# Attention times a gated dense block on one Trainium2 core: products with values in three blocks a pair of heads instead of four

## The chip, the cores and the metric

The kernel runs on one core of a Trainium2 chip. A core has a matrix engine (TensorE, PE in the profile, with PEld for its weight loads), a vector engine (VectorE, DVE), an engine for activations (ScalarE, ACT), a general one (GpSimd, POOL) and SyncE (SP), from whose queue all transfers of this kernel are issued. Each engine works through its own instructions in order. The metric is the device time of one execution in microseconds (us); lower is better.

## The reference

The input x has 2048 rows of 640 numbers. It is normalized row by row, and the result goes into two branches whose outputs are multiplied:

```python
xn = _layernorm(x, axis=-1)
s = _A_ref(xn, A_wqkv, A_wo)                               # attention
g = _silu(_B_ref(xn, B_w1, B_b1, B_w2, B_b2))              # dense block
return x + s * g
...
# attention: H = 32 heads of Dh = 20, window W = 256
mask = (idx[:, None] - idx[None, :] >= 0) & (idx[:, None] - idx[None, :] < W)
p = _softmax(jnp.where(mask, q @ k.T * Dh ** -0.5, -1e9))
return (p @ v).reshape(B, S, D) @ wo
# dense block: 640 -> 1536 -> 640
r = max(xn @ w1 + b1, 0)
return (r * r) @ w2 + b2
```

All data are 32-bit floats. With a window of 256, a tile of 128 queries meets three tiles of 128 keys: its own and the two before it.

## The kernel before

**Precision by parts.** Matrix products run in a reduced 32-bit form, so most operands are split into a high and a low part and three products are added (high x high, high x low, low x high).

**Three stages.** The first normalizes and transposes x, computes the values v for all heads and the first 128 columns of q and k, and stores them in device memory. The second is a loop of *steps* (line 1186), which does attention and, between its products, nearly everything else. The third multiplies the attention result with `wo`, gates it and writes the output (`out_filler`, line 1114).

**Steps.** Heads go in 16 pairs, each pair through 16 tiles of 128 rows. Step `s` computes the scores of one tile of queries (`scores`, line 470) and their row maxima on VectorE (`maxima`, line 482). Every fourth step the maxima of four tiles are turned on TensorE, negated and stored into two extra rows of q (`max_rows`, line 488). `LAG` = 9 steps later the same scores are computed transposed, keys by queries, with the maxima subtracted by those rows (`scores_t`, line 510); ScalarE takes the exponential and GpSimd sets the part outside the window to zero with one or two masks (`exps`, line 522, instructions on lines 524, 525 and 527). This leaves one probability tile for each block of keys `kb`, kept in `pts` in a ring of 8 buffers (tag `p32`).

**Products with values.** `PLAG` steps after the exponentials of the fourth, eighth, twelfth and sixteenth tile of a pair, `values(p, g)` (line 532) multiplies the last four probability tiles with v. The results of 8 tiles of queries lie in one accumulator `ot` of four column groups; two tiles share a column group, and a block of keys adds to up to three tiles. A 21st column of ones beside v's 20 columns gives the sums of the softmax. `evac` then copies two column groups to SBUF (line 551) and posts one store into `o_d[g]` (line 552); posted stores are issued by `post_all` (line 564) from SyncE's queue, which waits there for the copy.

**Two streams and the filler.** Score products and nearly all others in the loop use only 64 of the 128 rows of TensorE, so two of them run side by side: the code keeps two streams with a model clock each (`clock[0]`, `clock[1]`), puts the first half of a product into one and its second half into the other. The value products use all 128 rows, so `values` brings both clocks together and adds `PV`, the time the code books for a block. Between the products of attention, a generator `filler` (line 827) emits the rest: q and k for the other heads, then the first layer (`hps`) and the second layer (`yps`) of the dense block. `fill(upto)` (line 1166) takes work from it until the model clock has come to a given point. `pace` (line 1164) is all booked work divided by the number of steps, and each step fills up to `(s + 1) * pace`, or to `(s + 1) * pace - PV` where a block of values follows (line 1226).

**The order at the end.** The last block of the second layer consists of 8 half-products: four tiles of rows, each in two halves of 320 columns, one bank of three for each. VectorE empties a bank (`ysb`, line 960). Ahead of each half-product the filler calls `late()` (line 878), which, counted by `j`, loads the first attention results back (`load`, line 1062: transfers `ob` and `sums`), and turns them into operands (`turn_out`, line 1077: VectorE and ScalarE). The inverse of the softmax sums comes from `invert` (line 1019), called in every step: from `stored(g) + 3` on it loads the sums of column group `g`, from `stored(g) + 5` on VectorE takes the reciprocal, and a transfer stores it. `tick` (line 718) releases the splitting of weights (ScalarE line 765 or 773, VectorE line 768 or 774) by step and by how loaded the step is taken to be.

Of the kernel before, what the change touches and what calls it, by code (L numbers as in the profile page):

```python
# [9 lines left out]
F32 = mybir.dt.float32  # L10
# [5 lines left out]
P = 128  # L16
# [8 lines left out]
NB = 4  # L25
# [14 lines left out]
WARM2 = 10  # L40
COST = {P: 0.067, 2 * P: 0.12, HALF: 0.147, 3 * P: 0.172, BT: 0.23}
SCALE = DH ** -0.5
PV = 1.57
PLAG = 2
NEG = -1.0e30
EPS = 1e-5
SETTLE = 0.45
# [10 lines left out]
def attn_mlp_kernel(ctx: ExitStack, tc, x, wqkv, wo, w1, b1, w2, b2, out):  # L58
# [470 lines left out]

    ot = po_.tile([P, 4, P], F32, tag="o", name="ops")  # L530

    def values(p, g):
        for kb in range(4 * g, 4 * g + 4):
            pt = pts.pop((p, kb))
            ts = range(kb, min(kb + 3, NT))
            same, other = [t for t in ts if t % 2 == kb % 2], [t for t in ts if t % 2 != kb % 2]
            parts = [same] if kb % 8 < 6 else [[t] for t in same]
            for part in parts + [other]:
                for hh in range(2):
                    if not part:  # L540
                        continue
                    t = part[0]
                    r0 = 32 * (2 * hh + t % 2)
                    c0 = t // 2 % 4
                    first = t % 8 < 2 and kb == max(0, t - 2) or kb == 0
                    nc.tensor.matmul(ot[r0:r0 + VW, c0:c0 + len(part), :], vps[p][:, kb // 4, kb % 4, hh, :], pt[:, hh, :].rearrange("p (t n) -> p t n", n=P)[:, t - kb:part[-1] - kb + 1:2, :], start=first, stop=part[0] == kb, skip_group_check=True)  # L546
        clock[:2] = [max(clock[:2]) + PV] * 2

        def evac():
            osb = at2.tile([P, 2, P], F32, tag="osb", name="osb")  # L550
            nc.scalar.activation(osb, ot[:, 2 * g % 4:2 * g % 4 + 2, :], AF.Copy)
            post(o_d[g][p], osb.rearrange("p e n -> p (e n)"))
        later(SOON, evac)


# [271 lines left out]
    def filler():  # L827
# [50 lines left out]
        def late():  # L878
            j = lates[0]
            lates[0] += 1  # L880
            if j >= 3:
                load(0)
            if j >= 4:
                load(1)
            if j >= 5:
                turn_out(0, 0)
            if j >= 6:
                turn_out(0, 1)
                load(2)

# [118 lines left out]
        return 4 * (u // 2) + u % 2 + 2 * t2  # L1009

    def stored(g):
        return NP * NT - NT + 4 * g + 3 + LAG + PLAG

    rec_d = [dram.tile([2, H, MT], F32, name=f"rec_{g}") for g in range(NB)]
    recs = {}
# [3 lines left out]
    def invert():  # L1019
        for g in range(NB):  # L1020
            over = state[2] >= 10 ** 6
            if not over and state[2] < stored(g) + 3:
                return
            if g not in recs:
                rows = o_d[g].rearrange("p (h r) n -> (p h) r n", h=2)
                recs[g] = at2.tile([P, P], F32, tag="rec", name="rec")
                for par in range(2):
                    nc.sync.dma_start(recs[g][64 * par:64 * (par + 1)], rows[:, 32 * par + DH].rearrange("h (j n) -> h j n", n=P))
            elif recs[g] is not None and (state[2] >= stored(g) + 5 if not over else True):
                nc.vector.reciprocal(recs[g], recs[g])  # L1030
                nc.sync.dma_start(rec_d[g].rearrange("a h (j n) -> (a h j) n", n=P), recs[g])
                recs[g] = None
# [128 lines left out]
    whole = [False]  # L1161
    fl = filler()
    steps = NP * NT + LAG + PLAG
    pace = (8 * (KC - 1) * 15 * COST[BT] + 4 * NB * (3 * 30 * COST[MT] + 4 * 18 * COST[HALF]) + NP * (2 * NT * COST[3 * P] + NB * PV)) / (steps - 1)

    def fill(upto):
        soon()
# [10 lines left out]
    with tc.manual_schedule(engines={E_.PE, E_.Activation, E_.DVE, E_.Pool, E_.SP}):  # L1178
# [7 lines left out]
        for s in range(steps):  # L1186
# [35 lines left out]
            issue(RATE)  # L1222
            flush()
            tick()
            if e and e[1] % 4 == 3:
                fill((s + 1) * pace - PV)
                values(e[0], e[1] // 4)
            else:
                fill((s + 1) * pace)
        finish()  # L1230
# [30 lines left out]
```

## Time and profile before

| What | Value |
|---|---|
| Median of 3 runs | 863.55 us (861.12 to 864.31) |
| Profiled execution | 860.56 us, of which 858.8 us are the span from first to last instruction |
| TensorE busy | 845.2 us, 98% of the span |
| VectorE, ScalarE, GpSimd busy | 455.7, 423.2, 323.0 us |
| Clock granted to TensorE | full over the whole span |
| Value products | 2112, in 64 blocks |
| Stretches of the span | first stage to about 150 us; steps with q and k to 268 us; steps with the dense block to 784 us; output products from 784 us |

How to read it: a "busy" engine has an instruction running; products are pipelined on TensorE, so their records overlap and a busy TensorE can still be fed more or less densely. In the order of time, each row gives start, length, engine, line, operation, what is written and read, and the count of instructions merged into the row. What stands in brackets is the idle time before it and what ended it. Names are those of the program: `ops` is the accumulator of the value products, `p` a probability tile, `sps` and `stps` the two forms of scores, `hps` and `yps` the two layers of the dense block, `wops` the output products, `osb` the copy of the attention result.

### The profile page before, as it was taken

What the parts mean: (1) busy time and instruction counts of PE and PEld (TensorE: products, weight loads), DVE (VectorE), ACT (ScalarE), POOL (GpSimd) and SP (SyncE); (2) the same over time, 40 slices, a digit from 0 to 9 for tenths busy, and PEclk for the clock granted to TensorE, in tenths of its full rate; (3) what the DMA queues carried; (4) which work ended last, traced back from release to release, by engine and by line L of the source; (5) the groups of instructions that cost most, each with busy time, mean ns of one, the idle gap of its engine ahead of it and who ended that gap; (6) DMA issues with size and microseconds to landing.
All of it is one profiled execution on the core that took longest, in us unless ns stands there. A gap on an engine that the chain in (4) does not pass through costs nothing. (4 is left out here: it accounts for less than half of the span.)

```text
span 858.8 us, 26512 instructions
## 1 busy us (share of the span) xinstructions
PE 845.2 (98%) x10640; PEld 790.8 (92%) x10640; DVE 455.7 (53%) x1348; ACT 423.2 (49%) x808; POOL 323.0 (38%) x652
## 2 busy tenths in 40 slices
PE   9999999999999999999999999999999999979998
PEld 8999999888888999999999989999999999979997
DVE  7652136655567545454455456655445455345764
ACT  5222114545556753753754654854744744752321
POOL 6010002333333543543543543643543543621443
PEclk9999999999999999999999999999999999999999
DMA  7998587877879563264265336485276284367992
GB/s 264 297 405 292 169 210 259 272 246 251 267 252 300 145 209 125 77 193 129 80 201 179 89 101 180 128 261 173 71 209 180 66 256 143 95 141 205 281 269 85
DMA packets 94371, 166.50 MB, mean 194 GB/s; under 512 B 10920, under 2 KB 43816, under 8 KB 93224
## 3 DMA queue, kind: packets, MB, share of 16 engines
q1 hardware_dynamic: 94248, 164.80, 62.7%
q8 instruction: 84, 1.38, 0.7%
q14 instruction: 39, 0.32, 0.1%
HBM read 93.66 MB, written 70.52 MB: 191 GB/s over the span
## 5 line engine op out<-in xcount | busy, mean ns | idle before, releaser
L486 DVE CUSTOM_DVE_ANT_0 junk<-sps,mask 128x384 bf16<-128x384 f32 (+2 forms) x512 | 272.5, 532 | 249.0 <-PE hps L468 71.9
L524 ACT ACTIVATE p<-stps 128x768 f32<-128x768 f32 (+2 forms) x256 | 197.3, 771 | 261.9 <-PE stps L518 211.8
L468 PE MATMUL yps<-w,hh 64*128 64x320 f32 x1536 | 230.1, 309 | 6.6 <-DVE ysb L960 6.2
L525 POOL TENSOR_SCALAR_AFFINE_SELECT p<-p 128x256 f32<-128x256 f32 x256 | 104.3, 407 | 333.7 <-ACT p L524 319.2
L468 PE MATMUL hps<-xb,w 64*128 64x256 f32 x2520 | 220.7, 283 | 0.0
L468 PEld LDWEIGHTS hps<-xb,w 64*128 64x128 f32 x2520 | 208.8, 187 | 5.5 <-issue 5.4
L468 PEld LDWEIGHTS yps<-w,hh 64*128 64x128 f32 x1536 | 186.0, 185 | 11.6 <-DVE ysb L960 8.0
L468 PE MATMUL yps<-w,hl 64*128 64x320 f32 x768 | 178.5, 310 | 0.0
L478 PE MATMUL sps<-ks,qs 60*128 60x384 f32 (+2 forms) x512 | 142.6, 341 | 0.2
L518 PE MATMUL stps<-qs,ks 62*128 62x384 f32 (+2 forms) x512 | 135.6, 331 | 0.0
L468 PEld LDWEIGHTS yps<-w,hl 64*128 64x128 f32 x768 | 117.7, 185 | 2.3 <-issue 2.3
L468 PE MATMUL qkps<-xT,wgkh 64*128 64x512 f32 x320 | 100.5, 395 | 0.0
L468 PE MATMUL qkps<-xT,wgqh 64*128 64x512 f32 x320 | 98.9, 393 | 0.0
L546 PE MATMUL ops<-p,vp 128*21 128x128 f32 (+1 forms) x2112 | 92.8, 313 | 0.0
L527 POOL TENSOR_SCALAR_AFFINE_SELECT p<-p 128x256 f32<-128x256 f32 x224 | 91.5, 409 | 0.0
L478 PEld LDWEIGHTS sps<-ks,qs 60*128 60x128 f32 x512 | 87.7, 185 | 2.6 <-DVE mt L486 1.3
L518 PEld LDWEIGHTS stps<-qs,ks 62*128 62x128 f32 x512 | 88.5, 187 | 0.4
L546 PEld LDWEIGHTS ops<-p,vp 128*21 128x21 f32 x2112 | 65.2, 100 | 22.0 <-issue 8.8
L228 PE MATMUL vps<-wv,xT 128*128 128x320 f32 x480 | 71.5, 308 | 0.0
L228 PEld LDWEIGHTS vps<-wv,xT 128*128 128x128 f32 x480 | 70.5, 188 | 0.1
L930 POOL TENSOR_TENSOR hl<-sq,hh 128x512 fp32r<-128x512 f32 x48 | 62.3, 1298 | 21.2 <-ACT sq L929 21.2
L599 PE MATMUL wops<-wo,oT 128*128 128x320 f32 x384 | 61.6, 309 | 0.7 <-DVE ysb L960 0.7
(104 smaller groups left out, 1167.5 us busy)
## 6 DMA issues: line engine op xcount, KB each, us to landing
ks<-k_d SPq DMA_DIRECT2D x64, 240.0 KB
qs<-q_d SPq DMA_DIRECT2D x64, 240.0 KB
xb<-xs SPq DMA_DIRECT2D x60, 256.0 KB
xs<-xT SPq DMA_DIRECT2D x8, 1280.0 KB
k_d<-shm SPq DMA_DIRECT2D x19, 512.0 KB
q_d<-shm SPq DMA_DIRECT2D x19, 512.0 KB
y<-ysb SPq DMA_DIRECT2D x28, 320.0 KB
o<-osb SPq DMA_DIRECT2D x64, 128.0 KB
```

Source lines behind the costliest of these rows:

```text
L228: nc.tensor.matmul(ps, xT[xp][b][:, c * BT + t * P: c * BT + (t + 1) * P], wv[wp][:, c, nh * HALF:(nh + 1) * HALF], start=first and m == 0 ...
L468: return nc.tensor.matmul(out, a[r], b_[r], skip_group_check=True, **kw)
L478: nc.tensor.matmul(ss[hh][:, :nk], qs[i][o, q * P:(q + 1) * P], ks[i][o, k0 * P:k0 * P + nk], start=True, stop=True)
L486: nc.vector.tensor_tensor_reduce(out=junk[:, :nk], in0=ss[hh][:, :nk], in1=mask[:, 3 * P - nk:], scale=1.0, scalar=-3.0e38, op0=ALU.add, o ...
L518: nc.tensor.matmul(tps[:, hh, :n], ks[i][o, kb * P:(kb + 1) * P], qs[i][o, kb * P:kb * P + n], start=True, stop=True)
L524: nc.scalar.activation(p32[:, :, :n], tps[:, :, :n], AF.Exp, scale=SCALE)
L525: nc.gpsimd.affine_select(p32[:, :, 0:P], p32[:, :, 0:P], pattern=[[0, 2], [1, P]], compare_op=ALU.is_ge, fill=0.0, base=0, channel_multip ...
L527: nc.gpsimd.affine_select(p32[:, :, 2 * P:], p32[:, :, 2 * P:], pattern=[[0, 2], [-1, P]], compare_op=ALU.is_gt, fill=0.0, base=0, channel ...
L546: nc.tensor.matmul(ot[r0:r0 + VW, c0:c0 + len(part), :], vps[p][:, kb // 4, kb % 4, hh, :], pt[:, hh, :].rearrange("p (t n) -> p t n", n=P ...
L599: nc.tensor.matmul(ps, a, b_, start=j == 0, stop=j == n - 1)
L930: nc.gpsimd.tensor_sub(hh[1][:, :BT], sq, f32(hh[0]))
```

## The change

The 16 probability tiles of a pair are multiplied with v in three blocks, of six, six and four, instead of four blocks of four, and a block runs one step behind the exponentials of its last tile instead of two. With it go:

- the copy out takes three, three and two column groups; the second of these wraps around the end of the accumulator and becomes two copies; stores are cut where the column groups belong to different `o_d[g]`, so a pair has five stores instead of four;
- the time booked for a block is 2.25, 2.25 and 1.42 us instead of 1.57;
- `stored(g)` and the steps from which `invert` acts are set anew, the buffer of the inverted sums becomes single, and a new inversion starts only when none is open;
- `late()` acts at other counts of half-products.

```diff
-PV = 1.57
-PLAG = 2
+CUTS = (0, 6, 12, NT)
+PVS = (2.25, 2.25, 1.42)
+PLAG = 1
...
-    def values(p, g):
-        for kb in range(4 * g, 4 * g + 4):
+    def values(p, i):
+        lo, hi = CUTS[i], CUTS[i + 1]
+        for kb in range(lo, hi):
...
-        clock[:2] = [max(clock[:2]) + PV] * 2
+        clock[:2] = [max(clock[:2]) + PVS[i]] * 2
 
         def evac():
-            osb = at2.tile([P, 2, P], F32, tag="osb", name="osb")
-            nc.scalar.activation(osb, ot[:, 2 * g % 4:2 * g % 4 + 2, :], AF.Copy)
-            post(o_d[g][p], osb.rearrange("p e n -> p (e n)"))
+            c0, c1 = lo // 2, hi // 2
+            osb = at2.tile([P, 3, P], F32, tag="osb", name="osb")
+            c = c0
+            while c < c1:
+                n = min(4 - c % 4, c1 - c)
+                nc.scalar.activation(osb[:, c - c0:c - c0 + n], ot[:, c % 4:c % 4 + n, :], AF.Copy)
+                c += n
+            for g in range(c0 // 2, (c1 + 1) // 2):
+                d0, d1 = max(c0, 2 * g), min(c1, 2 * g + 2)
+                post(o_d[g][p, :, (d0 - 2 * g) * P:(d1 - 2 * g) * P], osb[:, d0 - c0:d1 - c0].rearrange("p e n -> p (e n)"))
...
-            if j >= 3:
+            if j >= 4:
                 load(0)
-            if j >= 4:
                 load(1)
-            if j >= 5:
+            if j >= 6:
                 turn_out(0, 0)
-            if j >= 6:
+            if j >= 7:
                 turn_out(0, 1)
                 load(2)
...
-        return NP * NT - NT + 4 * g + 3 + LAG + PLAG
+        return NP * NT - NT + min(c for c in CUTS if c >= 4 * (g + 1)) - 1 + LAG + PLAG
...
-            if not over and state[2] < stored(g) + 3:
+            if not over and state[2] < stored(g) + 2:
                 return
             if g not in recs:
+                if any(r is not None for r in recs.values()):
+                    return
                 rows = o_d[g].rearrange("p (h r) n -> (p h) r n", h=2)
-                recs[g] = at2.tile([P, P], F32, tag="rec", name="rec")
+                recs[g] = at2.tile([P, P], F32, tag="rec", bufs=1, name="rec")
...
-            elif recs[g] is not None and (state[2] >= stored(g) + 5 if not over else True):
+            elif recs[g] is not None and (state[2] >= stored(g) + 4 if not over else True):
...
-            if e and e[1] % 4 == 3:
-                fill((s + 1) * pace - PV)
-                values(e[0], e[1] // 4)
+            if e and e[1] + 1 in CUTS:
+                i = CUTS.index(e[1] + 1) - 1
+                fill((s + 1) * pace - PVS[i])
+                values(e[0], i)
```

More of the change, by code (lines that the diff above doesn't have):

```diff
@@ L1163, in attn_mlp_kernel @@
     steps = NP * NT + LAG + PLAG
-    pace = (8 * (KC - 1) * 15 * COST[BT] + 4 * NB * (3 * 30 * COST[MT] + 4 * 18 * COST[HALF]) + NP * (2 * NT * COST[3 * P] + NB * PV)) / (steps - 1)
+    pace = (8 * (KC - 1) * 15 * COST[BT] + 4 * NB * (3 * 30 * COST[MT] + 4 * 18 * COST[HALF]) + NP * (2 * NT * COST[3 * P] + sum(PVS))) / (steps - 1)
     def fill(upto):
```

## The prediction

> **What bounds the kernel now.** I read the page first (shares, clock, chain, costliest groups), then the busy time by stretch, then TensorE's instructions in order of time around blocks of value products, then the waits near the end.
>
> ```profile
> span 858.8 us, 26512 instructions
> PE 845.2 (98%) x10640; PEld 790.8 (92%) x10640; DVE 455.7 (53%) x1348; ACT 423.2 (49%) x808; POOL 323.0 (38%) x652
> PEclk9999999999999999999999999999999999999999
> PE 9%; DVE 0%; issue 0%
> PE wops L599 8%; PE yps L468 1%; PE ops L546 0%; DVE res L1151 0%; DVE ysb L960 0%; DVE res L1153 0%
> L546 PE MATMUL ops<-p,vp 128*21 128x128 f32 (+1 forms) x2112 | 92.8, 313 | 0.0
> ```
> ```profile
> 268.00:735.00 467.00, 465.14 (x7188) 437.49 (x7186) 245.69 (x841) 270.86 (x528) 212.49 (x447) 1.00 0.52 154
> 735.00:784.00 49.00, 43.38 (x621) 40.16 (x618) 18.02 (x36) 26.16 (x47) 16.38 (x31) 1.00 0.59 154
> 784.00:858.80 74.80, 70.56 (x480) 70.30 (x480) 46.57 (x64) 19.12 (x28) 31.26 (x30) 1.00 0.74 208
> ```
>
> TensorE (PE) is busy 98% of the span at full clock, and in the long middle, 268 to 735 us, for 465.14 of 467.00 us (first column the length, second PE, then weight loads, VectorE, ScalarE, GpSimd). No engine beside it is over 53%. So time is gained here only by making TensorE's stream shorter, and lost only by making TensorE wait. "Busy" hides one thing that the change is about: how densely products follow each other. For that I go to the order of time, one step without values and one with a block:
>
> ```profile
> 736.69 0.34 PE L478 MATMUL sps<-ks,qs 60*128 60x384 f32 x1
> ...
> 737.16 2.15 PE L468 MATMUL hps<-xb,w 64*128 64x256 f32 x32
> 739.08 0.34 PE L478 MATMUL sps<-ks,qs 60*128 60x384 f32 x1
> ...
> 739.26 0.34 PE L518 MATMUL stps<-qs,ks 62*128 62x384 f32 x1
> ...
> 739.55 0.71 PE L468 MATMUL hps<-xb,w 64*128 64x256 f32 x8
> 740.19 1.50 PE L546 MATMUL ops<-p,vp 128*21 128x256 f32 x32
> 741.62 0.38 PE L468 MATMUL hps<-xb,w 64*128 64x256 f32 x1
> 741.63 0.44 PE L478 MATMUL sps<-ks,qs 60*128 60x384 f32 x1
> 741.84 0.28 PE L468 MATMUL hps<-xb,w 64*128 64x256 f32 x1
> 741.91 0.34 PE L518 MATMUL stps<-qs,ks 62*128 62x384 f32 x1
> 741.96 0.34 PE L478 MATMUL sps<-ks,qs 60*128 60x384 f32 x1
> 742.09 0.28 PE L468 MATMUL hps<-xb,w 64*128 64x256 f32 x1
> 742.14 0.34 PE L518 MATMUL stps<-qs,ks 62*128 62x384 f32 x1
> 742.21 1.94 PE L468 MATMUL hps<-xb,w 64*128 64x256 f32 x28
> ```
>
> Columns: start, length, engine, line, operation, count. Ordinary products use 64 of the 128 rows each, two streams side by side; the value products (L546) use all 128 rows and 21 columns. In a plain run 32 products of 256 columns start within 2.15 - 0.28 = 1.87 us, 0.060 us apart. From 736.69 to 737.16 lie four score products and two of these: (0.47 - 0.12) / 4 = 0.088 us a score product.
>
> **The price of a block's edges.** From 739.55 to 742.21, 2.66 us, TensorE does 8 + 3 products of 256 columns (11 x 0.060 = 0.66), four score products (0.35) and one block: the block takes 2.66 - 1.01 = 1.65 us. Its 32 products start within 1.50 - 0.27 = 1.23 us, 0.040 apart, so 32 cost 1.27. The rest, 0.38 us, is paid for going into the full-row form and back: 0.21 us from the start of the last ordinary product (739.55 + 0.71 - 0.28 = 739.98) to 740.19, 0.20 us from the last value product's start (741.42) to 741.62, and 741.62 to 742.21, 0.59 us for work that goes in 0.53 elsewhere. A lower bound takes only the two gaps, less what an ordinary and a value product would need (0.41 - 0.10 = 0.31), less 0.06 because both streams restart together: 0.25 us. I take 0.35, near the upper row, since that one counts everything from the last undisturbed product to the next, and keep 0.25 to 0.38.
>
> [...]
>
> **The change part by part.**
> Blocks: 48 instead of 64 over 16 pairs; the 2112 value products, their weights and shapes stay. 16 x 0.35 = 5.6 us less on the engine that is the bound (4.0 to 6.1).
>
> One step behind instead of two: a block's last probabilities must be ready one step sooner. What that needs, once as usual and once the worst of the last steps of a block to be (6th, 12th, 16th of a pair):
>
> ```profile
> 346.57 0.34 PE L518 MATMUL stps<-qs,ks 62*128 62x384 f32 x1
> 348.40 0.41 POOL L527 TENSOR_SCALAR_AFFINE_SELECT p<-p 128x256 f32<-128x256 f32 x1
> 349.24 0.34 PE L518 MATMUL stps<-qs,ks 62*128 62x384 f32 x1
> ...
> 544.20 0.48 PE L518 MATMUL stps<-qs,ks 62*128 62x384 f32 x2
> 546.85 0.98 POOL L527 TENSOR_SCALAR_AFFINE_SELECT p<-p 128x256 f32<-128x256 f32 x1
> 546.93 0.34 PE L518 MATMUL stps<-qs,ks 62*128 62x384 f32 x1
> ```
>
> Usually GpSimd's second mask ends at 348.81, 2.24 us after the scores began at 346.57. A block starts 740.19 - 739.26 = 0.93 us behind its step's scores; one step later that is 349.24 + 0.93 = 350.17, so 1.36 us to spare. The worst is ready at 547.83, wanted at 547.86. And a block goes through its steps in order: of 48 products the last step's come after 40, another 40 x 0.04 = 1.6 us. Waiting of TensorE: 0; if that cover went, every late microsecond would cost one per block, 48 times. A block now holds seven probability tiles at its start (six of its own, one newer) where six were held, of eight buffers, so the exponentials wait for none.
>
> ScalarE, SyncE, planner:
>
> ```profile
> L551 ACT ACTIVATE osb<-ops 128x256 f32<-128x256 f32 x64 | 24.3, 379 | 5.6 <-PE ops L546 5.6
> L524 ACT ACTIVATE p<-stps 128x512 f32<-128x512 f32 x16 | 9.6, 599 | 28.1 <-PE stps L518 28.1
> L564 SPq DMA_DIRECT2D o<-osb x64: 319/343/666, 154.9 to 777.8; - x64
> SPq L564 <- ACT osb L551: 189.9, 54, 7.0
> ```
>
> Copies out stay 64: one of three column groups, one of one, two of two a pair. By 0.38 us for 256 columns and 0.60 for 512, 384 columns are about 0.49 and 128 about 0.27 (estimates), together 1.52 a pair against 4 x 0.38 = 1.52: 0. Stores rise from 64 to 80, 16 x 0.34 = 5.5 us on SyncE, which in that queue waits 189.9 us for these copies anyway: 0. Queued behind a block's second store is at times the pair of row stores for the maxima; their readers come three steps (over 7 us) later, so 0.34 us more is covered. The planner books 2.25 us for six steps; such a step then lasts some 0.96 + 2.25 = 3.2 us instead of 2.4 and the next carries less filler. The work is the same, and the rows show no wait that depends on even steps: 0. One step fewer in all, and a filler about a step ahead at the end: 0 by itself, since steps only order TensorE's stream.
>
> The end: the loads and turns of the first output tiles move one or two half-products later, as does the first inverted sum's turn in VectorE's queue.
>
> ```profile
> 758.98 0.56 PE L468 MATMUL yps<-w,hh 64*128 64x320 f32 x3 [1.74 <-DVE ysb L960]
> 772.49 0.41 PE L468 MATMUL yps<-w,hh 64*128 64x320 f32 x1 [3.01 <-DVE ysb L960]
> 768.11 1.56 DVE L1087 TENSOR_TENSOR ob<-ob,sums 128x512 f32<-128x512 f32 x2 [2.40 <-DMA sums<-rec]
> 771.21 0.83 DVE L774 TENSOR_TENSOR wo4l<-raw,wo4h 128x640 fp32r<-128x640 f32 x1 [1.53 <-ACT wo4h L773]
> 771.95 0.48 DVE L960 TENSOR_TENSOR ysb<-yps,yin 128x320 f32<-128x320 f32 x1
> ```
> ```profile
> 783.92 70.65 PE wops L599 x480
> ```
>
> Here TensorE waits 1.74 + 3.01 us for a bank, because VectorE, which empties it at 771.95, had stood 2.40 us for a transfer and 1.53 us for ScalarE in front of it. The transfer still has two half-products between its issue and the turn, so I expect a wait of the same size, one product later: 0, with -4.8 (all gone) to +4.8 (as much again) as its ends. The output products behind it start at 783.92 and take 70.65 us, in both kernels.
>
> Sum: 860.56 us (the profiled execution; span 858.8 and 1.8 around it) - 5.6 = 855.0. That execution lies 3.0 under the median of the runs, 863.55 (861.12 to 864.31), so against the median: **857.9 us**, 0.65% less.
>
> **Rivals.**
> 1. The waits at the end vanish. For it: they hang on order in VectorE's queue, which is what the moved thresholds touch. Against: the sums still come by the same chain of store, load, reciprocal, store, load. 857.9 - 4.8 = 853.1.
> 2. They grow and eat the gain: the turn now stands one half-product from the output products, and the second column group's inversion comes two steps later (step 263 for 261). 857.9 + 4.8 = 862.7, within 0.5%.
> 3. Slower: TensorE waits for the masked probabilities at the blocks. ScalarE's queue in a step behind a block holds an exponential, the longer copy, perhaps a weight split and the row copies; if GpSimd then ends its masks more than 1.36 + 1.6 = 3.0 us later than now, TensorE stands. From 9.9 / 48 = 0.21 us a block on, the gain of 5.6 turns into 0.5% loss; at 0.4 us it is 857.9 + 19 = 877. Against it: the worst of today is ready before the block even starts.
> 4. It doesn't do what it says, since the edges overlap something: the two gaps are measured start to start, so at least 0.25 us each is real, 4.0 us.
>
> **Chances.** My forecast, with the end unchanged: 0.50, its own range 855 to 861 (edge bounds, and 1.5 us of runs apart). Rival 1: 0.15. Rival 2: 0.20. Rival 3: 0.13. Rival 4's low end is inside the forecast; 0.02 is left for anything else. For this kernel 0.5% is 4.3 us, about what measurement tells from no change, so "faster" means under 859.2: 0.42 of the forecast's 0.50 and all of rival 1, 0.57. Within 0.5%: 0.08 and rival 2, 0.28. Slower: 0.15. The range takes in rivals 1 and 2 and leaves out rival 3: 852 to 864.5.
>
> **What would show it.** Right: 48 blocks, the six-step ones some 1.9 us from first to last start, gaps of 0.20 to 0.21 at their edges, output products starting some 5 to 6 us sooner than 783.9, no row "PE ops" waiting on GpSimd. Wrong: idle time ahead of L546 with GpSimd's mask as releaser (rival 3); longer waits of the second linear layer's products for VectorE between 735 and 784 (rival 2); or edges that grow when blocks are longer.

## The result, and the profile after

The changed kernel takes 873.08 us (median of 4 runs, 871.04 to 876.32), the kernel before 863.32 us (median of 4, 861.12 to 864.31). The ratio is 1.0119 (95% interval 1.0101 to 1.0137): 1.2% slower, where 0.65% faster was forecast. The profiled execution took 874.08 us, with a span of 872.4.

The page of the changed kernel, the lines that answer to those shown of before (lines of the code have moved: values L548, scores L479 and L519, filler L469, output products L608, maxima L487):

```profile
span 872.4 us, 26530 instructions
PE 850.6 (98%) x10640; PEld 797.7 (91%) x10640; DVE 451.9 (52%) x1348; ACT 422.7 (48%) x808; POOL 321.2 (37%) x652
PEclk9999999999999999999999999999999999998999
PE 85%; DMA 6%; issue 3%; DVE 2%; ACT 2%; POOL 1%; SPq 0%; DVEq 0%; POOLq 0%
L548 PE MATMUL ops<-p,vp 128*21 128x128 f32 (+1 forms) x2112 | 89.6, 313 | 0.0
```

The shares have not changed, and no engine became a second bound. Two things have: one slice near the end has less than full clock, and transfers stand in the chain that ended last. By stretches (columns as before: length, TensorE, weight loads, VectorE, ScalarE, GpSimd, granted clock):

```profile
268.00:747.00 479.00, 474.37 (x7316) 447.70 (x7314) 247.99 (x846) 275.11 (x539) 218.44 (x456) 1.00 0.51 151
747.00:787.50 40.50, 37.02 (x519) 33.90 (x516) 15.93 (x32) 22.22 (x38) 13.23 (x26) 1.00 0.46 122
787.50:872.40 84.90, 74.54 (x480) 73.06 (x480) 41.51 (x64) 19.03 (x28) 28.37 (x30) 0.95 0.77 208
```

The 480 output products took 74.8 us before and take 84.9 now, at a mean clock of 0.95: 10.1 us of the loss stand in this one stretch. In the middle TensorE stood still for 479.00 - 474.37 = 4.6 us against 467.00 - 465.14 = 1.9. To compare at equal work, I added up the columns of TensorE's products in each trace, every form at its rate, and took the difference of the times at which the same sum is reached (after less before):

| Time in the kernel before, us | 27 | 279 | 363 | 513 | 599 | 747 | 774 | 797 | end |
|---|---|---|---|---|---|---|---|---|---|
| Difference, us | +1.6 | +2.7 | +3.1 | +3.1 | +5.6 | +5.5 | +2.1 | +10.6 | +13.6 |

Instead of falling by 5.6 us, the difference rises in the steps by 3.9 (from +1.6 to +5.5), and by 8 at the end. The +1.6 at 27 us lies in the first stage, which the change doesn't touch; of the kernels below, the profiled executions of e7 and e15 show 1.5 us of it too and those of the others at most 0.4, so it comes and goes with the execution.

**The steps.** TensorE of the changed kernel in order of time (start, length, line, operation, count; in brackets the idle time before):

```profile
406.93 0.41 PE L479 MATMUL sps<-ks,qs 60*128 60x384 f32 x2
...
407.28 0.76 PE L469 MATMUL hps<-xb,w 64*128 64x256 f32 x9
407.96 2.17 PE L548 MATMUL ops<-p,vp 128*21 128x128 f32 x56
410.06 0.38 PE L469 MATMUL hps<-xb,w 64*128 64x256 f32 x1
410.07 0.44 PE L479 MATMUL sps<-ks,qs 60*128 60x384 f32 x1
...
410.40 0.34 PE L479 MATMUL sps<-ks,qs 60*128 60x384 f32 x1
...
410.65 1.34 PE L469 MATMUL hps<-xb,w 64*128 64x256 f32 x18
411.72 0.33 PE L479 MATMUL sps<-ks,qs 60*128 60x384 f32 x1
...
411.96 0.44 PE L479 MATMUL sps<-ks,qs 60*128 60x384 f32 x1
```

The longest block has 56 products in one run, and its edges look as before: from the start of the last ordinary product (407.28 + 0.76 - 0.28 = 407.76) to the first value product 0.20 us. But the step with the block lasts from 406.93 to 410.07, 3.14 us, and the next one only to 411.72, 1.65 us. Over all pairs the medians are 3.16 us for the steps that end in a six-step block and 1.63 to 1.68 for the steps behind them; before, the medians of all 16 steps of a pair lay between 2.26 and 2.60. VectorE at that place:

```profile
410.63 0.56 DVE L487 CUSTOM_DVE_ANT_0 junk<-sps,mask 128x384 bf16<-128x384 f32 x1 [2.06 <-PE hps L469]
...
411.34 0.56 DVE L487 CUSTOM_DVE_ANT_0 junk<-sps,mask 128x384 bf16<-128x384 f32 x1
411.83 0.08 DVE L487 DVE_READ_ACCUMULATOR2_ANT mt<- 128x1 f32 x1
412.18 0.56 DVE L487 CUSTOM_DVE_ANT_0 junk<-sps,mask 128x384 bf16<-128x384 f32 x1 [0.27 <-PE hps L469]
```

VectorE had nothing to do for 2.06 us during the long step, and then needs 0.71 us (410.63 to 411.34) for each of two maxima. The scores of a tile lie in two banks. The second is free again at 411.83 + 0.08 = 411.91, and the second score product of the next tile starts right behind, at 411.96. The short step has become a race that VectorE loses. In the kernel before the two maxima of a tile start 410.59 - 409.88 = 0.71 us apart as well, but its median steps have 2.26 us and more for them:

```profile
409.88 0.56 DVE L486 CUSTOM_DVE_ANT_0 junk<-sps,mask 128x384 bf16<-128x384 f32 x1 [0.94 <-PE stps L518]
410.59 0.56 DVE L486 CUSTOM_DVE_ANT_0 junk<-sps,mask 128x384 bf16<-128x384 f32 x1
```

Who waited for the maxima in the whole changed kernel (us, times):

```profile
  PEld sps L479: 6.1, 18
  PE sps L479: 1.2, 4
```

The same view of the kernel before:

```profile
  PEld sps L478: 1.3, 4
```

That is 7.3 us against 1.3 by name. Stalls like the one above, of some 0.1 us, aren't named in this view.

**The end.** VectorE of the changed kernel behind 794 us, in order of time:

```profile
799.17 0.95 DVE L1040 RECIPROCAL rec<-rec 128x128 f32<-128x128 f32 x1 [7.14 <-DMA rec<-o]
800.04 1.22 DVE L1161 TENSOR_TENSOR res<-wops,yq 128x320 f32<-128x320 f32 x3
805.87 0.69 DVE L1097 TENSOR_TENSOR ob<-ob,sums 128x512 f32<-128x512 f32 x1 [4.61 <-DMA sums<-rec]
```

TensorE at the same place:

```profile
794.18 1.92 PE L608 MATMUL wops<-wo,oT 128*128 128x320 f32 x12
...
796.23 0.31 PE L608 MATMUL wops<-wo4h,oT 128*128 128x320 f32 x1
800.62 1.67 PE L608 MATMUL wops<-wo,oT 128*128 128x320 f32 x5 [4.07 <-DVE res L1161]
```

And the busy times of two stretches there, columns as above:

```profile
795.00:801.00 6.00, 1.93 (x12) 1.69 (x11) 1.83 (x4) 0.00 (x0) 0.45 (x1) 0.89 0.44 128
801.00:806.00 5.00, 5.00 (x20) 5.00 (x20) 0.39 (x2) 0.00 (x0) 2.06 (x3) 0.50 1.03 220
```

The reciprocal of the last column group's sums stands in VectorE's queue and waits 7.14 us for the load of these sums. Behind it in the same queue is `res`, which empties the banks of the output products. So TensorE stands for 4.07 us, although no output product needs that reciprocal yet. In the kernel before the same reciprocal waits 0.29 us:

```profile
789.41 0.95 DVE L1030 RECIPROCAL rec<-rec 128x128 f32<-128x128 f32 x1 [0.29 <-DMA rec<-o]
```

TensorE's clock in the changed kernel is at half when it goes on: 20 products from 801 to 806 us, where the spacing at 794.18, (1.92 - 0.31) / 11 = 0.146 us, makes 34. The granted clock of short stretches is 1.00 up to 799.6 us, 0.73 from there to 799.8 and 0.50 behind it; 0.50 up to 806.4, 0.70 from there to 806.6 and 1.00 behind it. So it was at half from about 799.7 to 806.5 us.

### The profile page after: what moved, and what is told of

Same layout as the page of the kernel before. It is cut to its first block, busy times and chain, and to the rows that moved or that the text cites. A ratio compares the mean times of both kernels' runs of the same rounds, so it can differ in the third digit from the quotient of the medians.

```text
span 872.4 us, 26530 instructions
## 1 busy us (share of the span) xinstructions
PE 850.6 (98%) x10640; PEld 797.7 (91%) x10640; DVE 451.9 (52%) x1348; ACT 422.7 (48%) x808; POOL 321.2 (37%) x652
## 4 chain that ended last, share of the span: by engine, by line
PE 85%; DMA 6%; issue 3%; DVE 2%; ACT 2%; POOL 1%; SPq 0%; DVEq 0%; POOLq 0%
PE hps L469 19%; PE yps L469 17%; PE qkps L469 13%; PE ops L548 9%; PE vps L229 8%; PE wops L608 5%; PE sps L479 5%; PE stps L519 5%; PE qkps L206 3%; DMA out_dram<-res 1%; DVE junk L487 1%; DMA rec<-o 1%; DMA rec<-rec 1%; PE tps L173 1%; DMA ks<-k_d 1%
## 5 line engine op out<-in xcount | busy, mean ns | idle before, releaser
L487 DVE CUSTOM_DVE_ANT_0 junk<-sps,mask 128x384 bf16<-128x384 f32 (+2 forms) x512 | 272.3, 532 | 263.8 <-PE sps L479 132.8
L469 PE MATMUL yps<-w,hh 64*128 64x320 f32 x1536 | 228.0, 310 | 5.5 <-DVE ysb L968 5.0
L469 PE MATMUL hps<-xb,w 64*128 64x256 f32 x2520 | 214.7, 282 | 0.0
L469 PEld LDWEIGHTS hps<-xb,w 64*128 64x128 f32 x2520 | 203.1, 187 | 3.8 <-issue 3.8
L469 PEld LDWEIGHTS yps<-w,hh 64*128 64x128 f32 x1536 | 182.9, 185 | 11.9 <-DVE ysb L968 8.0
L469 PE MATMUL yps<-w,hl 64*128 64x320 f32 x768 | 175.6, 309 | 0.0
L479 PE MATMUL sps<-ks,qs 60*128 60x384 f32 (+2 forms) x512 | 134.0, 340 | 1.6 <-DVE mt L487 1.2
L519 PE MATMUL stps<-qs,ks 62*128 62x384 f32 (+2 forms) x512 | 126.1, 337 | 1.0 <-DMA qs<-mrow 1.0
L469 PEld LDWEIGHTS yps<-w,hl 64*128 64x128 f32 x768 | 115.3, 185 | 1.6 <-issue 1.5
L469 PE MATMUL qkps<-xT,wgqh 64*128 64x512 f32 x320 | 99.5, 393 | 0.0
L469 PE MATMUL qkps<-xT,wgkh 64*128 64x512 f32 x320 | 98.8, 394 | 0.0
L548 PE MATMUL ops<-p,vp 128*21 128x128 f32 (+1 forms) x2112 | 89.6, 313 | 0.0
L479 PEld LDWEIGHTS sps<-ks,qs 60*128 60x128 f32 x512 | 81.9, 185 | 7.7 <-DVE mt L487 6.1
L548 PEld LDWEIGHTS ops<-p,vp 128*21 128x21 f32 x2112 | 66.8, 101 | 18.6 <-issue 6.6
L519 PEld LDWEIGHTS stps<-qs,ks 62*128 62x128 f32 x512 | 78.9, 187 | 1.5 <-issue 1.3
L608 PE MATMUL wops<-wo,oT 128*128 128x320 f32 x384 | 64.4, 318 | 6.7 <-DVE res L1161 6.1
```

Of the source, the lines that this page charges most:

```text
L469: return nc.tensor.matmul(out, a[r], b_[r], skip_group_check=True, **kw)
L479: nc.tensor.matmul(ss[hh][:, :nk], qs[i][o, q * P:(q + 1) * P], ks[i][o, k0 * P:k0 * P + nk], start=True, stop=True)
L487: nc.vector.tensor_tensor_reduce(out=junk[:, :nk], in0=ss[hh][:, :nk], in1=mask[:, 3 * P - nk:], scale=1.0, scalar=-3.0e38, op0=ALU.add, o ...
L519: nc.tensor.matmul(tps[:, hh, :n], ks[i][o, kb * P:(kb + 1) * P], qs[i][o, kb * P:kb * P + n], start=True, stop=True)
L608: nc.tensor.matmul(ps, a, b_, start=j == 0, stop=j == n - 1)
```

## The experiments

Times below are medians; "against before" is the difference to the kernel before on the same chip in the same group of runs, and for the changed kernel it is 873.08 - 863.32 = +9.8 us.

| Kernel | Median, us | Ratio to before (95%) | Against before, us |
|---|---|---|---|
| e1_early_block | 868.25 | 1.0071 (1.0046 to 1.0095) | +5.4 |
| e2_two_recs | 868.49 | 1.0078 (1.0054 to 1.0103) | +5.6 |
| e3_early_block_two_recs | 867.17 | 1.0062 (1.0036 to 1.0089) | +4.3 |
| e4_before_uneven | 875.13 | 1.0148 (1.0128 to 1.0168) | +12.3 |
| e5_before_one_behind | 862.55 | 1.0005 (0.9993 to 1.0017) | 0.0 |
| e6_before_one_rec | 862.32 | 0.9999 (0.9986 to 1.0011) | -0.2 |
| e7_four_blocks | 869.95 | 1.0090 (1.0073 to 1.0107) | +7.4 |
| e8_eight_blocks | 892.11 | 1.0345 (1.0323 to 1.0367) | +29.6 |
| e9_old_counts | 877.31 | 1.0177 (1.0148 to 1.0205) | +14.5 |
| e10_early_two_recs_old_counts | 862.61 | 1.0003 (0.9989 to 1.0018) | -0.2 |
| e11_old_counts_load_table | 861.65 | 0.9984 (0.9966 to 1.0003) | -1.2 |
| e12_one_behind_load_table | 859.94 | 0.9978 (0.9966 to 0.9989) | -2.9 |
| e13_six_blocks_tail_in_order | 858.81 | 0.9953 (0.9937 to 0.9969) | -4.7 |
| e14_four_blocks_tail_in_order | 866.08 | 1.0040 (1.0025 to 1.0055) | +2.6 |
| e15_changed_load_table | 870.73 | 1.0082 (1.0055 to 1.0109) | +7.2 |
| e16_early_load_table | 865.42 | 1.0021 (1.0000 to 1.0041) | +1.9 |

### Are uneven steps the cost?

The theory: a block that ends late makes its step long and the next one short, and the short one waits for VectorE. The first edit lets the filler stop earlier in the steps with a block, so that steps come out even; nothing else of the changed kernel moves.

```diff
-            fill((s + EARLY_FILL) * pace)
+            i = CUTS.index(e[1] + 1) - 1 if e and e[1] + 1 in CUTS else None
+            fill((s + (EARLY_FILL if i is None else min(EARLY_FILL, max(0.0, 1 - PVS[i] / pace)))) * pace)
```

> The changed kernel with one thing more: in a step that ends with a block, the filler ahead of the block is cut so that scores, filler and the booked block fit into one pace (2.4 us); a six-step block then follows its step's scores at once. Theory A (short steps): in the changed kernel a step with a six-step block lasts 3.16 us and the next one 1.66 us, in which VectorE cannot finish the row maxima, so TensorE waits for them (7.3 us in 22 waits against 1.3 us in 4 before). With even steps that waiting falls to about 1 to 2 us and the time from 873.1 to 866 to 868 us. Rival B (the loss inside the steps is chance in the order of VectorE's queue): 871.5 to 874.5 us. The output phase stays slow in both (about 85 us from the first output product to the end).

The second goes the other way: the kernel before, with its blocks of four half a block late.

```diff
-                fill((s + 1) * pace - PV)
+                fill((s + 1) * pace - PV / 2)
```

> The kernel before, blocks of four untouched, but half of a block's booked time (0.785 us) is left out where the step's filler is cut ahead of it, so that a step with a block lasts about 0.8 us too long and the next is as much shorter, as in the changed kernel. Theory A: TensorE's waiting for the maxima rises from 1.3 us to 10 to 20 us (64 short steps at 0.15 to 0.33 us), time 870 to 880 us. Rival B: 861 to 865 us.

Measured: evened, the changed kernel is 868.25 us, 4.4 us better against before; its steps with and behind a six-step block have medians of 2.66 to 2.67 and 2.08 to 2.18 us. Made uneven (medians of 2.98 to 3.25 and 1.60 to 1.64 us), the kernel before is at 875.13, 12.3 us worse, and by the comparison at equal work its loss grows all along the steps, to +13.9 us at 747. Who waited for the maxima in the evened kernel:

```profile
  PEld sps L479: 3.9, 9
```

And in the uneven kernel before, beside 1.3 us in 4 places when it is even:

```profile
  PEld sps L478: 7.9, 28
```

What follows: uneven steps cost time, and in the kernel before the whole loss lies in the steps, 12.3 / 64 = 0.19 us a block. In the changed kernel evening is worth 4.4 / 48 = 0.09 us a block, but not all of that was found in the steps. By the comparison at equal work it brings 0.9 us up to 747 (+3.0 us there for e1, against 5.5 - 1.6 = 3.9 for the changed kernel without its first stage), 2.0 us between e2 and e3, and 3.3 us between e15 and e16 further down. e1 gives part of its gain away again, since TensorE waits 2.40 us in it for a row of maxima to land, against 1.00 in the changed kernel. And its output stretch, which the edit doesn't touch, takes 80.5 us instead of 84.9, so a part of the 4.4 us stands at the end.

The typical pair shows the price of short steps without such waits. I took the time of the 16 steps beyond what their products need undisturbed (0.060 us for 256 columns; the value products are the same in every pair). The median over 15 pairs is 1.46 us before, 1.48 after and 1.24 with even steps: in the typical pair the uneven steps took back all that the rest of the change had saved there.

### What one buffer for the inverted sums costs at the end

The theory: with one buffer and one inversion at a time, the last group's load goes out too late, and the reciprocal that waits for it holds up VectorE. The edit gives odd groups a second buffer and drops the rule that only one may be open; then the same with even steps.

```diff
-                if any(r is not None for r in recs.values()):
-                    return
-                recs[g] = at2.tile([P, P], F32, tag="rec", bufs=1, name="rec")
+                recs[g] = at2.tile([P, P], F32, tag="rec", bufs=1, name="rec") if g % 2 == 0 else f32(at2.tile([P, 3 * P], BF16, tag="junk", bufs=1, name="rec"))[:, :P]
```

> The changed kernel with the inversion of the softmax sums as before in one respect: two buffers (the second in space of the maxima's scratch, which is free by then) and no rule that one inversion must be closed before the next opens. Theory C (one buffer makes the tail late): the load of the last sums waits 5.2 us for the store of the ones before, VectorE stands 7.1 us at its reciprocal, TensorE 4.1 us for VectorE and then runs at half clock for some 5 us; with two buffers this goes, the output phase falls from 85 to 75 to 77 us and the time from 873.1 to 863 to 866 us. Rival D (the tail is late because the steps themselves end late, whatever the buffers): 870 to 873 us, with the same wait at another reciprocal.

> Both of the above. If A and C hold and are independent: 856 to 860 us, faster than the kernel before (863.3) by the 5.6 us that were forecast for 16 fewer edges of blocks, less some. If the edges save nothing in truth: 862 to 865 us.

The counterpart takes the second buffer away from the kernel before:

```diff
+                if any(r is not None for r in recs.values()):
+                    return
-                recs[g] = at2.tile([P, P], F32, tag="rec", name="rec")
+                recs[g] = at2.tile([P, P], F32, tag="rec", bufs=1, name="rec")
```

> The kernel before with one edit: one buffer for the inverted sums, and an inversion opens only when none is open. Theory C: the third or fourth reciprocal waits for its load behind the store before it, with VectorE standing 4 to 7 us and TensorE 2 to 4 us at the start of the output phase, 866 to 871 us against 862.9. Rival D (the tail of the changed kernel is slow because its steps end late, and one buffer does no harm to the kernel before): 862 to 864.5 us.

Measured: two buffers alone bring the changed kernel to 868.49 us, 4.2 better against before; its output stretch is 79.1 us instead of 84.9, with a wait of 2.7 us for `res` instead of 6.1 in all. But the kernel before loses nothing with one buffer. And with both cures at once 4.3 us stay, although the output stretch is back at 74.9: TensorE of that kernel (e3) now stands ahead of a product of the second layer.

```profile
780.24 0.90 PE L469 MATMUL yps<-w,hh 64*128 64x320 f32 x4 [4.18 <-DVE ysb L968]
```

VectorE in the same order of time shows why:

```profile
776.36 1.56 DVE L1095 TENSOR_TENSOR ob<-ob,sums 128x512 f32<-128x512 f32 x2 [4.43 <-DMA rec<-rec]
777.84 0.69 DVE L1099 TENSOR_TENSOR oT<-ob,oT 128x512 fp32r<-128x512 f32 x1
```

The turn of the first attention results waits 4.43 us for the stored reciprocals, and the copy of a bank (`ysb`) is queued behind it. So the wait was moved more than removed, and one buffer is a cost only in the company of other parts of the change. (e3 also spread widely, 864.1 to 873.6 us over 10 runs.)

### The counts of half-products at which the first results are loaded and turned

The theory: the moved counts of `late()` are what puts the turn in front of a needed copy. The edit restores the counts of before in the changed kernel (e9), and in the one with even steps and two buffers (e10):

```diff
-            if j >= 4:
+            if j >= 3:
                 load(0)
+            if j >= 4:
                 load(1)
-            if j >= 6:
+            if j >= 5:
                 turn_out(0, 0)
-            if j >= 7:
+            if j >= 6:
                 turn_out(0, 1)
                 load(2)
```

> The changed kernel with one part undone: the counts of half-products at which the first attention results are loaded and turned are those of before (3, 4, 5, 6 instead of 4, 4, 6, 7). Theory E (turning one half-product later puts VectorE's wait for the transfer in front of a bank that TensorE needs, and delays the first output products): the output products start 2 to 4 us sooner, 868 to 871 us against 873.1. Rival F (the tail depends on the inversions alone): 872 to 875 us.

> Blocks of six, six and four, placed early in their step, two buffers for the inverted sums, and the counts of before. Theory E: the wait of 4.4 us for VectorE shortly before the output products goes, 861 to 863 us against 867.2 with the later counts. Rival F: 866 to 868 us.

Measured: in the changed kernel the old counts make it worse, 877.31 us, +4.7 against the changed kernel's own loss. The longest wait of TensorE in e9, in the view of waits (total, times, longest):

```profile
PE stps L519 <- ACT p L525: 8.0, 1, 8.0
```

VectorE of e9 at that place:

```profile
775.83 1.56 DVE L1098 TENSOR_TENSOR ob<-ob,sums 128x512 f32<-128x512 f32 x2 [9.61 <-DMA ob<-o]
```

And ScalarE:

```profile
776.55 0.63 ACT L1099 ACTIVATE oT<-ob 128x512 fp32r<-128x512 f32 x1 [7.49 <-DVE ob L1098]
...
778.80 0.79 ACT L525 ACTIVATE p<-stps 128x768 f32<-128x768 f32 x1
```

VectorE waits for a transfer, ScalarE's turn waits for VectorE, the next exponential is queued behind the turn, and TensorE's next scores wait for the exponential, 8.0 us in one piece. So the counts alone aren't the cause. Yet with even steps and two buffers the same edit brings 4.5 us (867.17 to 862.61). The end is one chain of store, load, reciprocal, store, load and turn, and each threshold is right only for given values of the others.

### One step behind, and the table of loaded steps

One step behind alone, in the kernel before:

```diff
-PLAG = 2
+PLAG = 1
```

> The kernel before with one edit: blocks of four run one step behind the exponentials instead of two. Theory (the probabilities are ready in time): no wait of TensorE for GpSimd's masks, 861 to 865 us against 862.9. Rival (part of the loss is the shorter lag): waits of the value products for GpSimd of 0.2 us or more a block, 870 us or more.

Measured: no difference (1.0005), and no wait worth the name for the masked probabilities (0.2 us, once). But at equal work it loses 4.3 us up to 747 and gets 2.7 back at the end. Between 513 and 599 us alone it loses 2.4. VectorE of e5 there:

```profile
546.71 1.38 DVE L768 TENSOR_TENSOR w<-raw,w 128x640 fp32r<-128x640 f32 x1 [2.35 <-ACT w L765]
548.01 0.54 DVE L486 CUSTOM_DVE_ANT_0 junk<-sps,mask 128x384 bf16<-128x384 f32 x1
```

A weight split waits 2.35 us for ScalarE, and a maximum is queued behind it. The planner (`tick`) holds such splits back in steps that it takes to be loaded, and it finds them by a fixed table: 0.5 is added where `s % 4 == 3`. With two steps behind, these are the steps in which ScalarE copies a block out. With one behind, or with blocks of six, they aren't. The next edits move the table to the steps that follow a block: in the kernel one step behind (e12), in the changed kernel (e15), in the one with even steps (e16), and in e10 (e11).

```diff
-            vload[0] = 0.2 * (s % 4 == 0) + 0.5 * (s % 4 == 3)
+            done = at_step(s - LAG - PLAG - 1)
+            vload[0] = 0.2 * (s % 4 == 0) + 0.5 * bool(done and done[1] + 1 in CUTS)
```

In e12, with blocks of four, the same is `0.5 * (s % 4 == 2)`.

> The kernel before with blocks of four one step behind (862.6 us), and the planner's table of loaded steps moved by one step with them. Theory G: the 3 us between 500 and 560 us go, 859 to 861 us. Rival H: 862 to 863.5 us.

> The changed kernel with one thing more: the planner's table of loaded steps moved to the steps in which the attention result is copied out. Theory G: two to three of the 9.8 us lost come from the unmoved table: 869.5 to 871.5 us against 873.1. Rival H: 872 to 875 us.

> The changed kernel with its blocks placed early in their step (868.3 us) and the moved load table; tail unchanged. Theory G: 864.5 to 866.5 us, the two gains adding. Rival H: 867 to 869.5 us.

> The same, and the planner's table of loaded steps is set to the steps in which the attention result is really copied out (the step behind a block) instead of every fourth step. Theory G (with the lag of one the copies meet the splitting of weights on ScalarE, VectorE then waits for ScalarE and TensorE for VectorE's row maxima, 2 to 3 us between 500 and 560 us): 858 to 861 us, faster than before. Rival H (those waits are of other origin): the same as without, 861 to 863 us.

Measured, each against its counterpart with the old table: e12 -2.9 us, e15 -2.5, e16 -3.5, e11 -1.0. In the changed kernel the weight loads' wait for the maxima falls with it (who waited, e15):

```profile
  PEld sps L479: 3.8, 13
```

It was 6.1 us in 18 places. So the table is a part of its own, and a share of the named wait for the maxima belonged to it and not to uneven steps: of e15's 7.2 us, even steps (e16) still take 5.3. At equal work, one step behind loses 1.6 us up to 747 with the moved table (e12) instead of 4.3 (e5), and the whole kernel is then even 0.2% faster than before. e11 got least: its trace shows a new wait of 2.78 us at the end, behind two reciprocals, and then a drop of the clock to 0.50 (last section).

### The edge, priced by itself

Two kernels like e2, with four blocks of four and with eight blocks of two:

```diff
-CUTS = (0, 6, 12, NT)
-PVS = (2.25, 2.25, 1.42)
+CUTS = (0, 4, 8, 12, NT)
+PVS = (1.57,) * 4
...
-CUTS = (0, 6, 12, NT)
-PVS = (2.25, 2.25, 1.42)
+CUTS = tuple(range(0, NT + 1, 2))
+PVS = (0.97,) * 8
```

> The kernel of the run with two buffers for the inverted sums (868.5 us), with the blocks as before: four of four steps, 1.57 us booked for each, still one step behind. This undoes the change of the blocks alone. If an edge costs 0.35 us and the short steps behind six-step blocks cost as much as 16 edges save (0.2 to 0.3 us a pair each way), the time stays at 867 to 870 us. If the edges save nothing, it falls by the 5 us of the short steps, to 862 to 864 us.

> The same with eight blocks of two steps, 0.97 us booked for each: 64 edges more than with four blocks, and steps that stay even. At 0.35 us an edge 22 us more than with four blocks (16 us at 0.25, 24 us at 0.38). If the edge is hidden by something else: within 5 us of the run with four blocks.

Measured: 64 more blocks cost 892.11 - 869.95 = 22.16 us, 0.346 us a block, with all that a block brings along; the prediction took 0.35. Against e2 the four blocks are only 1.8 us slower, and this pair doesn't isolate the edge. At equal work the two are level at 747 us (+4.4 for e2, +6.1 for e7, 1.5 of it from the first stage): e2 has fewer edges but uneven steps. Behind that, e7 waits 4.4 us for a bank ahead of the output products, and e2 2.7 us among them.

### All parts together

The last wait at the end was the reciprocals of the later groups, which stand in VectorE's queue before the copies. In e13 they come only behind the last step, on top of e11; e14 is e13 with four blocks of four, each booked at 1.57 us.

```diff
-            elif recs[g] is not None and (state[2] >= stored(g) + 4 if not over else True):
+            elif recs[g] is not None and (g == 0 and state[2] >= stored(g) + 4 or over):
```

> The version with blocks of six, six and four placed early, two buffers, the counts of before and the moved load table (861.7 us), and the second and third reciprocal only after the last step, so that VectorE does not stand at them in front of a bank of the second layer. Theory: its last wait of 2.8 us and the reduced clock behind it (0.83 to 0.71 from 768 to 786 us) go: 856 to 859 us, clear of the kernel before. Rival (another wait takes the place): 860 to 863 us.

> The same with four blocks of four at 1.57 us each. If what an edge costs reaches the total time once the tail is in order, this is 4 to 6 us slower than the run with six, six and four: 860 to 865 us. If not, within 2 us of it.

Measured: e13 takes 858.81 us, a ratio of 0.9953 (0.9937 to 0.9969): it is 0.5% faster than the kernel before, and 1.6% faster than the changed one. TensorE's waits in e13, as total, times and longest:

```profile
PE wops L608 <- DVE res L1160: 2.8, 3, 2.3
PE stps L519 <- DMA qs<-mrow: 2.1, 1, 2.1
...
PE yps L469 <- DVE ysb L969: 1.3, 1, 1.3
...
PE sps L479 <- DVE mt L487: 0.8, 2, 0.5
```

e14 takes 866.08 us: with the same code otherwise, six, six and four are 7.3 us faster than four times four. The forecast for the edges was 5.6. In the median pair the steps of e14 cost 0.28 us more, which is 4.5 us over 16 pairs. The traces also differ at the end (4.1 us of waiting for `ysb` against 1.3), so 7.3 isn't the price of edges alone. And in the two profiled executions the steps as a whole are level (at 747 us +0.3 for e13, +0.4 for e14), because e13 loses about 3 us in a single pair, to a wait of 2.09 us and a slower clock behind it (0.50 from 389 to 391 us, last section).

Part of e13's 4.7 us is the clock, too. The mean granted clock of every execution is on record: of the 77 executions of the kernel before beside the experiments, the 43 with 0.996 or less take 862.0 to 867.0 us and the 10 with 0.999 or 1.000 take 860.1 to 861.8. The profiled execution before is of the second kind, which accounts for most of the 3.0 us by which the prediction found it under the median. Four of e13's seven have 1.000. Between executions at 0.999 or more on the same chip, four of each, the medians differ by 860.7 - 858.2 = 2.5 us.

## Why the prediction was wrong

**What was right.** The edge: 0.346 us measured by itself, 0.35 in the sum, and in the median pair the steps of e13 and e14 differ by 0.28 us, 4.5 over 16 pairs, where the bounds were 4.0 to 6.1. The block itself: same products, same gaps (the second block of a pair has 56 products and not 48, which changes no term). The masks: rival 3, 0.21 us a block and more of waiting for masked probabilities, didn't happen. In the changed kernel the value products' weight loads waited for GpSimd 0.6 us in 3 places, and e5, one step behind alone, is at 1.0005. In e13 such waits are 3.2 us in 13 places; in no kernel here do the value products themselves wait for GpSimd by name. Rival 4 is out with the measured edge. ScalarE's copies (24.3 us in all before, 22.3 after) and SyncE's 16 more stores show no cost of their own, though no run isolates the stores.

**What failed**, along a chain of kernels that begins at +9.8 us and ends at -4.7:

| Edit | Kernels | Against before, us |
|---|---|---|
| even steps | changed to e1 | +9.8 to +5.4 |
| second buffer | e1 to e3 | +5.4 to +4.3 |
| counts of half-products | e3 to e10 | +4.3 to -0.2 |
| table of loaded steps | e10 to e11 | -0.2 to -1.2 |
| later reciprocals behind the last step | e11 to e13 | -1.2 to -4.7 |

1. *"The planner books 2.25 us for six steps; such a step then lasts some 0.96 + 2.25 = 3.2 us instead of 2.4 and the next carries less filler. The work is the same, and the rows show no wait that depends on even steps: 0."* The 3.2 us were right to 0.04; the 0 was wrong: with even steps the same kernel is 4.4 us faster. In three pairs of kernels that differ by this alone, 0.9, 2.0 and 3.3 us of it were found in the steps themselves. In the kernel before no wait depended on it because its steps were even. The rows that price it were in its trace: two maxima 0.71 us apart in a step, against two banks of scores. A step of 1.65 us leaves 1.65 - 1.42 = 0.23 us for the rest of the way from a score to the next one, a step of 2.4 leaves 0.98.
2. *"One step fewer in all, and a filler about a step ahead at the end: 0 by itself, since steps only order TensorE's stream."* They also order the planner. Its table names steps by number, and a block that comes a step earlier, or every six steps, makes it name the wrong ones: 2.5 us in the changed kernel, 2.9 in the kernel before one step behind. I had worked out what the move costs on the engines and not what it does to the code that plans by the step's number.
3. The end: *"I expect a wait of the same size, one product later: 0, with -4.8 (all gone) to +4.8 (as much again) as its ends."* The output stretch alone grew by 10.1 us. Rival 1's opposite came. Rival 2 named the right place in part, VectorE's queue, but stopped at the start of the output products. The single buffer, and with it the last group's reciprocal in front of `res`, was in the diff, and my working had no term for it. Of the 0.15 for slower, 0.13 stood on rival 3 and 0.02 on anything else; the slower result came from elsewhere. The size was out of the bounds for another reason too: I took "as much again" for the worst, and a wait of 4.07 us brought a drop of the clock to 0.50. At half rate from 800.62 to 806.5 that is (806.5 - 800.62) / 2 = 2.9 us more.

The end isn't a sum of these parts. A second buffer is worth 4.2 us alone and 1.1 with even steps; the old counts lose 4.7 us in the changed kernel and win 4.5 two edits later; a single buffer costs nothing in the kernel before. What is shown is that the parts at the end together make 9.1 us of the chain above (1.1 + 4.5 + 3.5). How they share it depends on the order in which they are taken away, and the smallest steps of the chain, 1.1 (e1 to e3) and 1.0 (e10 to e11), lie within the intervals of their ratios.

What stays open: where the 1.6 us in the first stage of the profiled execution come from, and which part of the 873.08 they are. TensorE also waits, once, for the row of maxima to land (`qs<-mrow`): 1.0 us in the changed kernel, 0.9 to 2.4 in ten of the twelve made from it, 0.8 in e4 and e12, and not at all in the kernel before; no run tried to remove it. Nor does a run set back by themselves the steps from which `invert` loads the sums and takes the reciprocals. And the 5.6 us of the edges didn't appear in full in any kernel against the one before: e13, with all parts mended, is 2.5 to 4.7 us faster.

## What to carry to other kernels

When an edit makes a piece of work longer and rarer, look at the step it leaves behind as well as at the saving: compare the shortest step with what every other engine must do in it, and count the buffers between. Look for tables and thresholds that name steps by number, since they keep their old meaning when work is moved. At the end of a kernel, list each in-order queue, and for each instruction that waits for a transfer ask what stands behind it and who needs that: a wait at the right place costs nothing (in the kernel before VectorE waits 6.99 us ahead of 750.46 for a load of sums, and TensorE has no wait there), a wait of 7.14 us in front of a bank's copy stopped the bounding engine for 4.07 us.

## What the runs showed of the hardware

TensorE's clock fell to half in or behind some waits, and in the changed kernel this made a wait of 4.07 us cost more than itself. There TensorE had stood still since 796.54 us, and the clock was 0.50 from 799.7 to 806.5 us (worked out above). In e11 the same came with a shorter wait. TensorE of e11 in order of time:

```profile
769.14 0.56 PE L469 MATMUL yps<-w,hh 64*128 64x320 f32 x3 [2.78 <-DVE ysb L969]
```

Its stretches of one us or less, with the granted clock in the column behind GpSimd's:

```profile
769.10:770.00 0.90, 0.85 (x12) 0.86 (x13) 0.90 (x2) 0.00 (x0) 0.00 (x0) 1.00 1.06 221
770.00:771.00 1.00, 1.00 (x16) 1.00 (x14) 0.95 (x2) 0.00 (x0) 0.00 (x0) 0.84 1.07 182
771.00:772.00 1.00, 1.00 (x10) 1.00 (x10) 0.00 (x0) 0.00 (x0) 0.00 (x0) 0.50 0.89 200
...
773.00:774.00 1.00, 1.00 (x8) 1.00 (x6) 0.00 (x0) 0.00 (x0) 0.00 (x0) 0.50 0.90 200
```

Here the wait was 2.78 us, and the half clock came when TensorE was already working again: 1.00 up to 770, 0.84 from there to 771 and 0.50 from 771 to 774 us. In e13 the half clock came behind a still shorter wait, in the steps. First TensorE in order of time, then a stretch of busy times:

```profile
387.16 0.44 PE L519 MATMUL stps<-qs,ks 62*128 62x384 f32 x2 [2.09 <-DMA qs<-mrow]
389.00:391.00 2.00, 2.00 (x28) 1.23 (x18) 0.00 (x0) 0.00 (x0) 0.28 (x1) 0.50 0.00 0
```

Yet 3.01 us of waiting ahead of 772.49 in the kernel before left the clock at full: its stretches from 769.4 to 772.4, 772.4 to 774 and 774 to 776 us all have 1.00. So on this kernel the length of a single wait doesn't decide, and no run shows what does. A wait as long as these, the shortest of which is 2.09 us, has to be priced with and without a slow stretch behind it.
